# Nine heads of projection ahead of the scores, with half of the stacks and the late modulation placed later

## The chip, the cores and the metric

The kernel runs on one core of a Trainium2 chip. The metric is the device time of one execution in microseconds. The span of a profile is the time from the first to the last instruction of the program; the execution's own time is a little longer.

## The reference, cut to what matters

A transformer block on one sequence of 2048 tokens with 1024 channels, all in float32. A vector `c` gives six modulation rows, `mod = silu(c) @ w_mod`. Then:

```python
h = layernorm(x) * (1 + ca) + sa
x = x + ga * A(h)          # attention with a memory, then @ wo
h = layernorm(x) * (1 + cb) + sb
x = x + gb * B(h)          # mixer over the tokens: gelu(w1) and w2
```

`A` has 32 heads of 32 channels and cuts the tokens into 4 segments of 512. In each segment and head it computes

```python
logits = qs @ ks.T * scale + mask          # causal
a_dot = softmax(logits) @ vs
a_mem = (phi(qs) @ M) / (phi(qs) @ z + 1e-6)
o = g * a_mem + (1 - g) * a_dot
M = M + phi(ks).T @ vs;  z = z + phi(ks).sum()
```

so that a segment reads the memory `M`, `z` of those before it.

## The kernel before, in words

The work falls into two halves. The attention, to about 1000 us, ends with the products with `wo`; the mixer after it multiplies by `w1` and `w2` in a seven-product scheme for 2x2 blocks (`mix`, L927) and isn't touched by the change.

**Tiles and heads.** Four heads form a group `g` (8 of them). A tile `t` is one group on one segment: 32 tiles, first all groups on segments 0 and 1 (`pr` 0, tiles 0 to 15), then all groups on segments 2 and 3 (`pr` 1). A head's number in the loop is n = 4t + h, from 0 to 127. Matmuls take their operands in a high and a low part, so one projection is three matmuls per chunk.

**One tile's steps.** `project(t, piece)` (L378): pieces 0 and 1 make keys and values of two halves of the tokens (`nps`, 48 matmuls of 256 columns each), piece 2 transposes the keys (`kps`), makes the queries (`qps`, 24 matmuls of 512 columns), and writes both, split in high and low parts by ACT and DVE, to `sg`, of which there is one buffer. Piece 3 prepares the values (`vp`, three buffers) and reads and updates the memory (`am`, three buffers). `stack(t, h)` (L368) copies a head's rows of `sg` to its operand `sk` with three DMAs on SP (L374 to L376). There are two sets of four `sk`, so tile t's stack for head h waits until the scores of tile t - 2, head h, have read the old one. `maxima(t, h)` (L468) computes scores `sx`, `sy`, `sz` on TensorE and their row maxima on DVE; every second head transposes the maxima (`nmps`, L486) and writes their negatives into `sk` by four small DMAs (`sk<-nt`, L493). `scores(t, h)` (L507) computes the transposed scores `a0`, `a1`, `a2`, from which ACT makes exponentials `p32`; POOL masks them, ACT and POOL split them in halves `ph` and `p32`. `values(t, h)` (L533) multiplies by `vp` into the one bank `pv`; after a tile's last head the result is transposed (`ops`, L564), copied to `ot` and stored to `oT` in HBM.

**The order of the program.** The loop at L691 runs over n. In each step it issues the scores of head n, the maxima of head n + 3 (`LEADS`), the values of head n - 2 (`VL`), and projection piece m = n + 8 (`LEADP`). Stacks 0 to 2 of a tile are issued behind its piece 2, stack 3 with piece 3. Other work hangs on the steps by `plan` and `later` (a fetch at one step, its use at a later one): tokens 1024 to 2047, whose h is made from `gaw` and stored to `hT1` (steps 0 to 45), the weights of a group (`rawv`, `rawq`: fetched, split, and kept in `wsp`, from step 8g - 13), the 32 chunks of the late modulation rows (`mod_fetch` loads 512 KB `rawm`, `mod_late` reduces it on DVE: steps 49 to 56, then every second step from 60), and wo's eight parts (`wo_fetch`, `wo_split`, from step `WO0` = 65, every sixth). For m from 59 to 66 the h of segments 2 and 3 is loaded back (`reload_h`, 16 times 512 KB), the first eight of them into the pages of segment 0, as soon as its last projection has read them. At m = 123 to 130 wo's parts take the pages over.

A scheduler takes this program and sets the order on each engine by a model of the times; an engine then works its list off strictly in order, waiting on semaphores. SP issues all DMAs from one list, too, so a DMA that waits for its source or for its target's last reader holds back all behind it.

**The products with wo.** `product(tt)` (L778) loads a block of 128 tokens of `oT` as `otr` (one buffer), splits it to `ots`, and TensorE makes `po` in two halves of 24 matmuls (L797); blocks 0 to 7 need tiles of `pr` 0 alone, block 8 needs tile 30 (group 7, segment 2), block 12 needs tile 31. The first products stand between the last heads of the attention.

Of the kernel before, what the change touches and what calls it, by code (L numbers as in the profile page):

```python
# [26 lines left out]
SHIFT = 14.0 * math.log(2.0)  # L27
NV = 97
FT = F // P
LEADP, LEADS, NSK = 8, 3, 8  # L30
XB = 4
VL = 2
ML0 = 36
HB = 3
WO0 = 65
WOS = 6
WCT = 5
LEADP = 8
LEADS = 3


def attention_and_mlp(ctx, tc, x, wq, wkv, wo, beta, w1, b1, w2, b2, c, wm_a, wm_b, out):
# [320 lines left out]
    NI = len(its)  # L363
    st = {}

    last_sk, last_nt = {}, {}

    def stack(t, h):  # L368


        sk = st[t]["sk", h] = skt[t % 2][h]
        skf = sk.bitcast(F32)
        src = st[t]["sg"].bitcast(F32)[32 * h:32 * h + 32]
        SY.dma_start(skf[0:32], src[:, 0:3:2])  # L374
        SY.dma_start(skf[32:64], src[:, 0:4:3])
        last_sk[t, h] = SY.dma_start(skf[64:96], src[:, 1:3])  # L376

    def project(t, piece):  # L378
        pr, g, seg = its[t]
# [20 lines left out]
        elif piece == 2:  # L400
# [19 lines left out]
            if seg < 3:  # L420
# [3 lines left out]
                A.activation(r, r, AF.Exp, scale=-1.0)  # L424
                d["pk"] = pj.tile([P, 4, 128], F32, tag="pk", bufs=1, name=f"pk{t}")
                V.scalar_tensor_tensor(d["pk"].rearrange("p a n -> p (a n)"), kf, 0.0, r, op0=ALU.max, op1=ALU.add)
            for h in range(3):
                stack(t, h)
        else:
            stack(t, 3)  # L430
            v = d["v32"][:, :, 0:128].rearrange("p a (h e) -> p a h e", h=4)
            vp = d["vp"] = b.tile([P, 4, 4, NV], BF16, tag="vp", bufs=3, name=f"vp{t}")
            r1 = pj.tile([P, 4, 4, 32], F32, tag="tmp", bufs=2, name=f"r1_{t}")
# [240 lines left out]
        later(6 * i, lambda i=i: load_gaw(i),  # L674
              6 * i + 3, lambda r, i=i: token_tile(8 + i), "V")
    for g in range(2, NG):
        n = 8 * g - 13
        plan(n, lambda g=g: W.__setitem__((0, g), {}))
        for kind, part, n0, n1 in (("v", 0, 0, 1), ("v", 1, 1, 3), ("q", 0, 2, 4)):
            later(n + n0, lambda g=g, kind=kind, part=part: fetch_part(g, kind, part),  # L680
                  n + n1, lambda r, g=g, kind=kind, part=part: split_part(g, kind, part, r), "A")
        plan(n + 4, lambda g=g: keep_w(g))
    for j in range(32):
        n = 49 + j if j < 8 else ML0 + 2 * j + 8
        later(n, lambda j=j: mod_fetch(j), n + 1, lambda r, j=j: mod_late(j, r), "V")
    plan(WO0 - 3, lambda: spread(gaw, 0))
    for i in range(8):
        n = WO0 + WOS * i
        later(n, lambda i=i: wo_fetch(i), n + 1, lambda r, i=i: wo_split(i, r), "G")

    for n in range(-LEADS, 4 * NI + VL):  # L691
        at(scores, n)
        at(maxima, n + LEADS)
        with behind(n, "P" if n - VL >= 64 else ""):
            at(values, n - VL)
        m = n + LEADP
        if 0 <= m + 4 < 4 * NI:
            t = (m + 4) // 4
            if its[t][:2] not in W:
                with tc.issue_after(last_sk[t - 2 if t > 16 else 0, 3].ins):  # L700
                    load_w(its[t][1], its[t][0])
        if m >= 8:
            at(project, m)
        if 59 <= m < 67:
            seg, ct = 2 + (m - 59) // 4, 2 * ((m - 59) % 4)
            with ExitStack() as s:
                if seg == 3:
                    s.enter_context(tc.issue_after((last_sk[15, 3] if ct < 4 else last_nt[14, 3]).ins))
                reload_h(seg, ct)
                reload_h(seg, ct + 1)  # L710
        if 4 * NI - 5 <= m < 4 * NI + 3:
            i = m - 4 * NI + 5
            for c in (2 * (i % 4), 2 * (i % 4) + 1):
                wop[c, i // 4] = new_page(f"wo{c}_{i // 4}")
                if c < 5 or i < 4:
                    SY.dma_start(wop[c, i // 4].bitcast(F32), wos[c, i // 4])
        for f, engines in todo.pop(n, ()):
            with behind(n, engines):
                f()
# [427 lines left out]
```

## Time and profile before

| | us |
|---|---|
| median of 3 runs | 2226.57 |
| lowest and highest | 2223.17, 2226.85 |
| the profiled execution | 2224.45 |
| its span | 2222.7 |
| PE busy | 2184.5 |
| DVE busy | 1673.2 |
| ACT busy | 1132.7 |
| POOL busy | 723.6 |

The engines are PE (TensorE matmul), PEld (its weight loads), DVE (VectorE), ACT (ScalarE), POOL (GpSimd) and SP, which issues the DMAs. An engine's idle time is written in brackets behind the instruction that ends it, with what released it. The granted clock is TensorE's share of full speed. Names have lost their numbers: `sx<-sk` is any head's first maxima matmul; where the text names a tile and head, they were found by counting the instructions of that line in the program's order. A busy PE isn't PE at its peak, since a matmul's end is modelled.

### The profile page before, as it was taken

What the parts mean: (1) busy time and instruction counts of PE and PEld (TensorE: products, weight loads), DVE (VectorE), ACT (ScalarE), POOL (GpSimd) and SP (SyncE); (2) the same over time, 40 slices, a digit from 0 to 9 for tenths busy, and PEclk for the clock granted to TensorE, in tenths of its full rate; (3) what the DMA queues carried; (4) which work ended last, traced back from release to release, by engine and by line L of the source; (5) the groups of instructions that cost most, each with busy time, mean ns of one, the idle gap of its engine ahead of it and who ended that gap; (6) DMA issues with size and microseconds to landing.
All of it is one profiled execution on the core that took longest, in us unless ns stands there. A gap on an engine that the chain in (4) does not pass through costs nothing.

```text
span 2222.7 us, 38130 instructions
## 1 busy us (share of the span) xinstructions
PE 2184.5 (98%) x13786; PEld 1881.3 (85%) x13786; DVE 1673.2 (75%) x3762; ACT 1132.7 (51%) x2050; POOL 723.6 (33%) x831
## 2 busy tenths in 40 slices
PE   8999999999999999999999999999999999999999
PEld 5988998889999999888888888888888888888887
DVE  7677777767777677664858766888888887869687
ACT  5476777755666666654636533533334242424232
POOL 2165766656767677553002200033330000000000
PEclk9999999999999999999999999999999999999999
DMA  7656665587566665664754686655556541414134
GB/s 287 193 172 195 183 185 160 169 297 246 167 195 203 199 206 176 192 227 133 232 204 185 227 318 255 246 225 207 214 203 222 199 153 60 142 57 147 57 124 152
DMA packets 175184, 423.05 MB, mean 190 GB/s; under 512 B 17524, under 2 KB 71828, under 8 KB 166036
## 3 DMA queue, kind: packets, MB, share of 16 engines
q1 hardware_dynamic: 174996, 420.61, 57.4%
q8 instruction: 110, 1.80, 0.3%
q14 instruction: 78, 0.64, 0.1%
HBM read 244.62 MB, written 125.06 MB: 166 GB/s over the span
## 4 chain that ended last, share of the span: by engine, by line
PE 82%; DVE 6%; DMA 5%; ACT 3%; issue 1%; POOL 1%; SPq 1%; DVEq 0%; ACTq 0%
PE mx L927 47%; PE nps L192 10%; PE qps L200 7%; PE po L797 6%; PE pv L549 3%; DMA otr<-oT 1%; PE a L515 1%; DMA sk<-sg 1%; PE sz L478 1%; PE sx L478 1%; POOL p L531 1%; PE a L522 1%; PE sy L478 1%; PE a L518 1%; PE up L460 1%
## 5 line engine op out<-in xcount | busy, mean ns | idle before, releaser
L927 PE MATMUL mx<-bU,sp 128*128 128x512 f32 x2352 | 534.7, 389 | 1.0 <-DVE ac L934 0.9
L927 PEld LDWEIGHTS mx<-bU,sp 128*128 128x128 f32 x2352 | 441.1, 188 | 94.1 <-issue 1.3
L119 ACT CAST sp<-wr 128x384 fp32r<-128x384 f32 (+2 forms) x408 | 217.2, 545 | 433.0 <-PE mx L927 354.8
L192 PE MATMUL nps<-wv,h 128*128 128x256 f32 x3072 | 430.9, 283 | 1.1 <-DVE h L122 0.7
L927 PE MATMUL mx<-bA,sp 128*128 128x512 f32 x1764 | 430.5, 389 | 0.0
L531 POOL TENSOR_TENSOR p<-p,ph 128x640 f16<-128x640 f32 x256 | 377.7, 1476 | 121.7 <-ACT ph L529 116.8
L192 PEld LDWEIGHTS nps<-wv,h 128*128 128x128 f32 x3072 | 402.7, 190 | 8.8 <-DVE h L122 1.8
L927 PEld LDWEIGHTS mx<-bA,sp 128*128 128x128 f32 x1764 | 331.2, 188 | 68.7
L122 DVE TENSOR_TENSOR sp<-wr,sp 128x384 fp32r<-128x384 f32 (+2 forms) x408 | 259.1, 646 | 28.9 <-ACT sp L119 28.7
L934 DVE TENSOR_TENSOR ac<-mx,ac 128x512 f32<-128x512 f32 x280 | 189.4, 685 | 85.1 <-PE mx L927 84.5
L200 PE MATMUL qps<-h,wq 128*128 128x512 f32 x768 | 196.4, 399 | 0.0
L529 ACT CAST ph<-p 128x1280 f16<-128x1280 f32 x128 | 161.1, 1258 | 49.7 <-POOL p L527 49.2
L797 PE MATMUL po<-wo,ots 128*128 128x512 f32 x768 | 179.7, 391 | 1.4 <-ACT ots L119 1.4
L527 POOL TENSOR_SCALAR_AFFINE_SELECT p<-p 128x256 f32<-128x256 f32 x256 | 135.5, 535 | 119.9 <-ACT p L524 70.4
L797 PEld LDWEIGHTS po<-wo,ots 128*128 128x128 f32 x768 | 143.4, 188 | 31.2 <-ACT ots L119 1.8
L927 PE MATMUL mx<-bB,sp 128*128 128x512 f32 x588 | 164.0, 389 | 0.0
L200 PEld LDWEIGHTS qps<-h,wq 128*128 128x128 f32 x768 | 140.5, 189 | 27.1
L927 PEld LDWEIGHTS mx<-bB,sp 128*128 128x128 f32 x588 | 110.4, 188 | 22.9
L934 DVE TENSOR_TENSOR cc<-mx,cc 128x512 f32<-128x512 f32 x140 | 94.9, 684 | 41.7 <-PE mx L927 41.6
L480 DVE CUSTOM_DVE_ANT_0 sz<-sz,mask 128x512 f32<-128x512 f32 x128 | 89.2, 697 | 47.8 <-PE sz L478 46.9
L480 DVE CUSTOM_DVE_ANT_0 sx<-sx,mask 128x128 f32<-128x128 f32 (+1 forms) x256 | 93.3, 365 | 35.2 <-PE sx L478 31.5
L516 ACT ACTIVATE p<-a,shift 128x512 f32<-128x512 f32 x128 | 88.0, 688 | 43.6 <-PE a L515 39.6
(207 smaller groups left out, 3193.9 us busy)
## 6 DMA issues: line engine op xcount, KB each, us to landing
sk<-sg SPq DMA_DIRECT2D x384, 128.0 KB
wr<-in_w_dram SPq DMA_DIRECT2D x28, 1024.0 KB
wr<-in_w_dram SPq DMA_DIRECT2D x32, 768.0 KB
bstu<-ucd SPq DMA_DIRECT2D x28, 768.0 KB
wsp<-wv SPq DMA_DIRECT2D x32, 512.0 KB
rawm<-in_wm_b_dram SPq DMA_DIRECT2D x32, 512.0 KB
wv<-wsp SPq DMA_DIRECT2D x32, 512.0 KB
pcd<-cc SPq DMA_DIRECT2D x14, 1024.0 KB
```

Of the source, the lines that this page charges most:

```text
L119: last_hi[0] = A.copy(hi, src)
L122: return lo_eng.tensor_tensor(lo, src, hi.bitcast(F32), op=ALU.subtract)
L192: T.matmul(ps[:, aa], h[:, j, 128 * tt:128 * tt + 128], wt[:, i, o:o + 256], start=(n == 0), stop=(n >= 6 * NK - 2), skip_group_check=True)
L200: T.matmul(ps, wt[:, i, o:o + 128], h[:, j], start=(k + n == 0), stop=(3 * k + n == 3 * NK - 1))
L480: marks[4 * t + h - LEADS, "V"] = V.tensor_tensor_reduce(o, o, mask[:, 384 - 128 * i:], 1.0, -3.0e38, op0=ALU.add, op1=ALU.max, accum_out= ...
L516: A.activation(p32[:, 0:512], b0, AF.Exp, scale=SCALE, bias=shift)
L527: G.affine_select(w, w, pattern=[[0, 2], [1, 128]], compare_op=ALU.is_ge, fill=0.0, base=0, channel_multiplier=-1)
L529: marks[n, "A"] = A.copy(hi, p32)
L531: marks[n, "G"] = G.tensor_tensor(lo[:, c], p32[:, c], hi[:, c], op=ALU.subtract)
L797: T.matmul(ps, os_[:, i, P * ct:P * ct + P], wop[ct, nh][:, j], start=(n == 0), stop=(n == 3 * NK - 1))
L927: T.matmul(ps, ops[q][:, i, P * k:P * k + P], b[:, j], start=(m == 0 and first), stop=(m == 3 * nk - 1), skip_group_check=True)
L934: V.tensor_tensor(d, ps, d, op=ALU.add)
```

## The change

The lead of the projections goes from 8 to 9 heads: project piece m = n + 9. With it go what is counted in m (weights of a group, the reload of h, wo's pages), and the weights' fetches by step number, one step earlier. A tile's third and fourth stack (from tile 2 on) no longer follow its own pieces 2 and 3, but are issued at m = 4t + 4 and 4t + 5, ahead of that step's projection. The first eight modulation chunks are fetched at steps 58 to 65 instead of 49 to 56, the others six steps later (66 to 112), and wo's parts four steps later (from 69). The wait that the reload of segment 3 is issued behind names stack 1 of tile 15 instead of stack 3.

```diff
-LEADP = 8
+LEADP = 9
-WO0 = 65
+WO0 = 69
...
-            for h in range(3):
+            for h in range(3 if t < 2 else 2):
                 stack(t, h)
         else:
-            stack(t, 3)
+            if t < 2:
+                stack(t, 3)
...
-        n = 8 * g - 13
+        n = 8 * g - 14
...
-        n = 49 + j if j < 8 else ML0 + 2 * j + 8
+        n = 58 + j if j < 8 else 50 + 2 * j
...
         m = n + LEADP
-        if 0 <= m + 4 < 4 * NI:
-            t = (m + 4) // 4
+        t = (m - 2) // 4
+        if 2 <= t < NI and m % 4 < 2:
+            stack(t, 2 + m % 4)
+        if 0 <= m + 3 < 4 * NI:
+            t = (m + 3) // 4
...
-                    s.enter_context(tc.issue_after((last_sk[15, 3] if ct < 4 else last_nt[14, 3]).ins))
+                    s.enter_context(tc.issue_after((last_sk[15, 1] if ct < 4 else last_nt[14, 3]).ins))
```

The scheduler makes new lists from this on every engine. Three places follow. In these rows the last number of a name is a buffer's; the one or two before it are tile and head, and `wv0_5` is a weight of `pr` 0, group 5.

On TensorE, around the first maxima of tile 9. Before:

```order
L549 MATMUL pv7_1_4548<-vp7_3658,p32_7_1_4279 128x65
L478 MATMUL sx_9_0_4755<-sk1_0_501 128x128
L478 MATMUL sx_9_0_4755<-sk1_0_501 128x256
L478 MATMUL sy_9_0_4760<-sk1_0_501 128x384
L522 MATMUL a2_7_3_4527<-sk1_3_504 128x256
```

With the change:

```order
L192 MATMUL nps10_1_4737<-wv0_5_1_1_4448,h0_6_423 128x256 x3
L192 MATMUL nps10_1_4737<-wv0_5_1_1_4448,h0_7_451 128x256
L519 MATMUL a1_8_0_4675<-sk0_0_497 128x384
L192 MATMUL nps10_1_4737<-wv0_5_1_1_4448,h0_7_451 128x256 x5
L479 MATMUL sx_9_0_4806<-sk1_0_501 128x128
L479 MATMUL sx_9_0_4806<-sk1_0_501 128x256
L479 MATMUL sy_9_0_4811<-sk1_0_501 128x384
```

The maxima stood among the values of tile 7, head 1, with 24 `nps` of tile 10 between them and the last `qps` of tile 9; now they stand behind all 96 `nps` of tile 10.

On SP, at the reload of segment 2 (`h2`) and the first stack of tile 14. Before:

```order
L359 DMA h2_5_7169<-hT1_66 128x1024
L359 DMA h2_6_7292<-hT1_66 128x1024
L359 DMA h2_7_7294<-hT1_66 128x1024
L374 DMA sk0_0_497<-sg14_6788 32x2x512
L567 DMA oT_57<-ot11_6669 128x512
L375 DMA sk0_0_497<-sg14_6788 32x2x512
```

With the change:

```order
L359 DMA h2_5_7096<-hT1_66 128x1024
L374 DMA sk0_0_497<-sg14_6723 32x2x512
L375 DMA sk0_0_497<-sg14_6723 32x2x512
L376 DMA sk0_0_497<-sg14_6723 32x1024
L359 DMA h2_6_7211<-hT1_66 128x1024
L359 DMA h2_7_7213<-hT1_66 128x1024
L575 DMA rawm2_8008<-in_wm_b_dram 128x1024
```

The stack stood behind all eight loads of `h2` and behind `rawm0` to `rawm3`; now it stands behind six of them and behind `rawm0` and `rawm1`, and `rawm3` to `rawm10` come after the reload of segment 3.

On TensorE, near the end of the attention, where tile 30's result is transposed. Before:

```order
L797 MATMUL po4_0_15452<-wo1_0_14143,ots4_15445 128x512
L797 MATMUL po4_0_15452<-wo2_0_14263,ots4_15445 128x512 x3
L797 MATMUL po4_0_15452<-wo3_0_14265,ots4_15445 128x512 x3
L564 MATMUL ops30_14948<-ident_90,am30_14118 128x128 x4
L522 MATMUL a2_31_2_14964<-sk1_2_503 128x256
```

With the change:

```order
L801 MATMUL po4_0_15452<-wo7_0_14433,ots4_15445 128x512
L801 MATMUL po4_1_15478<-wo0_1_14521,ots4_15445 128x512 x3
L801 MATMUL po4_1_15478<-wo1_1_14523,ots4_15445 128x512 x3
L565 MATMUL ops30_14948<-ident_90,am30_14057 128x128 x4
L523 MATMUL a2_31_2_14964<-sk1_2_503 128x256
```

The transposes stood inside the first half of block 4's product, with 36 of its matmuls left before block 8's; now they stand inside its second half, with 18 left.

More of the change, by code (lines that the diff above doesn't have):

```diff
@@ L29 @@
 FT = F // P
-LEADP, LEADS, NSK = 8, 3, 8
+LEADP, LEADS, NSK = 9, 3, 8
 XB = 4
```

## The prediction

> **What bounds the kernel now.** I began with the page's first lines and then took the span in stretches (columns of a stretch: its length, busy time of PE, PEld, DVE, ACT, POOL with instruction counts, granted TensorE clock, DMA share, GB/s).
>
> ```profile
> span 2222.7 us, 38130 instructions
> PE 2184.5 (98%) x13786; PEld 1881.3 (85%) x13786; DVE 1673.2 (75%) x3762; ACT 1132.7 (51%) x2050; POOL 723.6 (33%) x831
> 450.00:500.00 50.00, 45.04 (x370) 40.18 (x370) 32.55 (x87) 27.34 (x51) 28.73 (x35) 0.95 0.88 299
> 550.00:600.00 50.00, 50.00 (x440) 46.46 (x440) 35.80 (x106) 32.10 (x55) 32.60 (x39) 1.00 0.51 139
> 1100.00:1150.00 50.00, 50.00 (x223) 41.40 (x222) 26.87 (x66) 19.48 (x37) 0.00 (x0) 1.00 0.65 222
> ```
>
> TensorE bounds both halves. The mixer (from 1050 us) is solid PE and none of its code is edited, so all that can change is the attention half, and there only time in which PE stands still or runs slowly. The stretch 450 to 500 us is the weakest: 5 us idle, a clock of 0.95, the most DMA.
>
> Next I took PE's waits, and the rows in time order (start, length, what, and in brackets the idle time ahead with its releaser):
>
> ```profile
> 135.16 0.47 PE L478 MATMUL sx<-sk 96*128 96x128 f32 x2 [2.33 <-issue]
> 319.53 0.47 PE L478 MATMUL sx<-sk 96*128 96x128 f32 x2 [0.74 <-DMA sk<-sg]
> 465.51 0.47 PE L515 MATMUL a<-sk 98*128 98x512 f32 x1 [0.74 <-DMA sk<-nt]
> 479.50 0.47 PE L478 MATMUL sx<-sk 96*128 96x128 f32 x2 [1.54 <-DMA sk<-sg]
> 491.29 0.61 PE L549 MATMUL pv<-vp,ph 128*128 128x97 bf16 x10 [0.43 <-ACT ph L529]
> 492.77 0.20 PE L549 MATMUL pv<-vp,p 128*128 128x65 bf16 x1 [0.87 <-POOL p L531]
> 495.10 0.51 PE L549 MATMUL pv<-vp,p 128*128 128x65 bf16 x6 [1.38 <-POOL p L531]
> 935.11 0.47 PE L478 MATMUL sx<-sk 96*128 96x128 f32 x2 [1.08 <-DMA sk<-sg]
> ```
>
> Four of them are a tile's first maxima (`sx`, head 0 of tiles 3, 9, 14 and 30, in the order of the program), which wait for the stacks; for tile 3 no releaser is named, but only four matmuls of projection part it from its `qps`. The other four lie in the weak stretch. The chain of waits there reads:
>
> ```profile
> 449.82 5.10 DMA rawm<-in_wm_b_dram
> 458.40 6.97 DMA sk<-nt
> 470.74 8.63 DMA sk<-sg
> 317.11 2.29 DMA sk<-sg
> 925.77 9.20 DMA sk<-sg
> 462.52 5.71 SPq L359 DMA_DIRECT2D h<-hT  x7
> ```
>
> A stack's DMA lands in 2.3 us when the queues are calm and in 8.6 to 9.2 us behind a burst of half-megabyte loads: modulation rows (`rawm`), weights and the reload of h. Then the stretches of 10 us show what the stall costs beyond the idle time:
>
> ```profile
> 130.00:140.00 10.00, 7.20 (x50) 6.61 (x51) 9.36 (x13) 6.94 (x11) 7.59 (x6) 0.83 1.01 297
> 470.00:480.00 10.00, 8.46 (x91) 8.12 (x88) 4.74 (x11) 4.99 (x8) 7.28 (x8) 1.00 0.84 290
> 490.00:500.00 10.00, 7.32 (x47) 6.21 (x46) 6.80 (x18) 6.25 (x12) 7.24 (x8) 0.73 0.97 358
> 500.00:510.00 10.00, 10.00 (x88) 9.55 (x88) 7.20 (x15) 5.56 (x10) 5.53 (x6) 0.93 0.72 168
> ```
>
> After two of the stalls the clock is held down: (0.17 + 0.27 + 0.07) x 10 = 5.1 us of TensorE work lost.
>
> **The change part by part.** Sums start from the profiled execution, 2224.45 us (span plus 1.75), 2.1 under the median 2226.57. No instruction is added or removed; what moves is places in queues. On SP that is 30 tiles x 2 stacks x 3 = 180 DMAs, each holding SP 0.6 us, now behind negative maxima and loads that stood after them; those go out sooner, since they no longer queue behind a stack that waits for its scores. The weights' fetches move one head with the projections that read them: nothing.
>
> *First maxima.* With nine heads of lead, all 96 `nps` matmuls of the next tile stand between a tile's last `qps` and its first `sx`; before there were 4, 24, 83 and 76 of them for tiles 3, 9, 14 and 30. One costs 0.114 us:
>
> ```profile
> 64.38 5.00 PE nps L192 x44
> ```
>
> So the stack's DMA gains 10.5, 8.2, 1.5 and 2.3 us of cover from these alone, for waits of 2.33, 0.74, 1.54 and 1.08 us. For tile 14 the queue helps as well: of the half-megabyte transfers from the last tokens' store on, 20 stood ahead of its first stack on SP, now 13, so 7 x 0.52 MB at the 358 GB/s of the row above is 10 us less to land first. All four waits go: **-5.7 us**. What is late next is the scores' wait for the negative maxima, below.
>
> *Clock.* The slow spell at 130 us follows tile 3's wait, the one at 490 us the burst. Both causes go: **-5.1 us**.
>
> *The weak stretch.* The other waits there, 0.74 + 0.43 + 0.87 + 1.38 = 3.4 us, are scores whose maxima landed 7 us late, and values behind an ACT and POOL that were held up in turn. Of the eleven `rawm` loads between the last tokens' store and the end of the reload of segment 3, two stay there and one goes just ahead; eight leave the stretch: **-3.4 us**. These loads, their `mod_late` on DVE and wo's split are not less work; they lie 6 heads (9 for the first eight) and 4 heads later, in a stretch like the 550 row, where DVE is 72% busy and DMA half. I cost them at nothing; without that cover eight DVE steps would have to be waited for, 8 x 1.2 us at most by this row (two steps):
>
> ```profile
> 512.29 2.32 DVE rawm L578 x2
> ```
>
> *Tail.* The last tile of segment 2 has to be transposed (`ops30`), stored and read back before the product of token block 8 (`po8`) can start. Columns as above:
>
> ```profile
> 1015.72 0.60 PE L564 MATMUL ops<-ident,am 128*128 128x128 f32 x4
> 1017.39 0.57 ACT L566 COPY ot<-ops 128x512 f32<-128x512 f32 x1
> 1019.11 0.38 SPq L567 DMA_DIRECT2D oT<-ot  x1
> 1023.68 0.37 SPq L781 DMA_DIRECT2D otr<-oT  x1
> 1028.36 0.73 PE L797 MATMUL po<-wo,ots 128*128 128x512 f32 x2 [1.37 <-ACT ots L119]
> 1046.27 104.55 PE po L797 x461
> ```
>
> That path takes 12.0 us from the end of `ops`, and PE waits 1.37 of them. In the new order 18 `po4` matmuls fewer stand between (18 now, 36 before), at 104.55 / 461 = 0.227 us each: 4.1 us less cover. The wait becomes 1.37 + 4.1 = 5.5 us, or 3.7 if the copy starts at once and the store isn't queued behind a load of x (1.07 and 0.72 us of slack in these rows). I take 4.5, so +3.1; and since 2.33 us of idle brought the clock down at 135 us, I add what that spell cost, 0.17 x 10 = 1.7: **+4.8 us** in all, bounds +2.3 and +5.8.
>
> The Trainium skill, "TensorE: Matmul & The Clock Gate", section "Part 1: The HAM clock gate (the "warmup" mystery)", says that the clock halves after a whole idle window of about 3.4 us, free-running. The row at 135.16, with 2.33 us of idle, disagrees with a whole idle window. By that rule a wait of 4.5 us need not hold one, the tail would cost 3.1, and the sum below would be 1.7 less.
>
> *Values.* Two values matmuls now stand close behind their own scores (tiles 5 and 11, head 2): by counting instructions 1.9 and 2.2 us. The shortest such distance now is
>
> ```profile
> 301.50 0.42 PE L522 MATMUL a<-sk 98*128 98x256 f32 x2
> 303.05 1.26 ACT L529 CAST ph<-p 128x1280 f16<-128x1280 f32 x1 [0.51 <-POOL p L527]
> 305.04 0.35 PE L549 MATMUL pv<-vp,ph 128*128 128x97 bf16 x4
> ```
>
> 3.1 us. So each waits about 1 us: **+2 us**; bounds 0 (PE may come late there anyhow) and +6, if the second half of `p` on POOL is waited for as well.
>
> *The single `sg` buffer.* A tile's third and fourth stacks still wait for the scores two tiles back, but are placed two heads later, and the next tile's write into `sg` on ACT and DVE must wait until they have landed. Behind that write on ACT are the exponentials, and PE's values wait for those. In the order of before under 5.3 us of PE work lie between those scores and the next `kps` in 3 tiles, now in 10, and in tiles 7 and 13 `kps` comes first. Issue (three at 0.6) and landing (2.3) need some 4.5. Before, ACT waited there once (answer on `sg`: us, times):
>
> ```profile
>   DMA sk<-nt: 4.2, 1
> ```
>
> The scheduler has put ACT's writes behind other work, so I take 1 us for each of tiles 7, 10 and 13: **+3 us**; bounds 0 and 3 x 4.2 = 12.6.
>
> *Three buffers.* `vp` and `am` of a tile are now rewritten one head after their last reader, before two. POOL's wait there (in sum, times, longest) is
>
> ```profile
> POOL vp L434 <- PE pv L549: 11.3, 8, 3.0
> ```
>
> and costs nothing while POOL, 65% busy in the 550 row, has the slack; bounds 0 and +3.0, one such wait on the path.
>
> Sum: -5.7 - 5.1 - 3.4 + 4.8 + 2 + 3 = -4.4, so 2224.45 - 4.4 = **2220.0 us**, 0.30% under the median.
>
> **The rivals.** *All covers hold*: nothing for values and `sg`, the tail at its lower bound: -14.2 + 2.3 = -11.9, 2212.5 us. For it: the mean distance from `qps` to `sx` grows from 11 to 18 us by counting. Against: ACT and POOL were as tight in the first half.
>
> *The clock stays up at the tail*: the wait at 479.50 left 1.00 in its row, so a wait alone need not lower it. Then the tail costs 3.1 and the time is 2218.3 us. The rule of the Trainium skill, named above, would allow this.
>
> *The wait moves*: each tile's scores need the negative maxima back in the stack. With later maxima the distance from the last maximum to its transposition falls (from 9.4 to 6.2 us on average in the first 16 tiles, and 9.9 to 5.6 after, by counting). If the first maxima no longer wait but the scores do, the 5.7 us come back: 2225.7 us. For it: the 0.74 at 465.51. Against: that one row is all there is of it.
>
> *Slower: the `sg` buffer decides.* The landing that rows show at 2.3 us rises to 7 to 9 behind loads. From about 5 us on, the seven tiles that newly fall under 5.3 us make ACT wait 4.2 us each, 29 us, and if PE passes on 45% of that (ACT is 55 to 64% busy in the 50 us rows of the attention), 13 us come on top: 2220.0 + 13 = 2233 us. For it: bursts in every second tile while weights are split. Against: three tiles had as little before, and ACT waited once.
>
> **How the numbers follow.** Forecast 2220.0 (2216 to 2222): 0.32. All covers hold: 0.12. Clock stays up: 0.08. The wait moves, from 2222.1 to 2231: 0.31. Slower: 0.17. A measurement of this kernel can tell some 0.2% from no change: 4.5 us, so faster is under 2222.1 and slower over 2231.0. Faster takes the first three, 0.52; same 0.31; slower 0.17. The range reaches from below the case with all covers to short of the slower one: 2210 to 2231, with about 0.05 left out below and 0.13 above; the upper bounds of tail, values, buffers and `sg` all together (2237.6), and those with the DVE steps, lie in what is left out.
>
> **What would show it.** In the new profile: no `sx` waiting for `sk<-sg` for over 0.5 us; clock 1.00 from 140 us to 1000 us; the former weak stretch with PE idle under 1.5 us and its longest `sk<-sg` on the chain hardly waited for; a wait of 3 to 5 us ahead of `po8` near 1015 to 1025 us, and a lowered clock behind it. ACT waiting for `sk<-sg` ahead of its `sg` write over 1 us in more than three tiles would make the slower case. PE waits in front of `a` for `sk<-nt` of over 4 us in sum would make the moved one. The forecast is wrong if the two slow-clock spells come back elsewhere in the first 500 us, or if the tail's wait is hidden.

## The result, and the profile after

| | before | after |
|---|---|---|
| median, us | 2224.56 (6 runs, 2220.15 to 2226.85) | 2231.80 (6 runs, 2230.38 to 2233.65) |
| ratio, 95% interval | | 1.0035 (1.0021 to 1.0048) |
| the profiled execution | 2224.45 | 2230.38 |

The change makes the kernel slower by 0.35%, 7 to 8 us; the forecast was 2220.0. The profiled executions differ by 5.9 us. The page of after begins:

```profile
span 2228.7 us, 38071 instructions
PE 2186.6 (98%) x13786; PEld 1883.1 (84%) x13786; DVE 1661.2 (75%) x3762; ACT 1133.7 (51%) x2050; POOL 721.2 (32%) x831
```

PE stands still for 2228.7 - 2186.6 = 42.1 us (before 38.2), and the same 13786 matmuls are busy 2.1 us longer. Where the idle time lies, a view by stretch shows (columns as in the prediction), first of before, then of after:

```profile
60.00:450.00 390.00, 379.73 (x3311) 347.02 (x3312) 282.84 (x822) 274.70 (x512) 225.95 (x261) 1.00 0.62 181
450.00:1045.00 595.00, 581.30 (x5034) 531.31 (x5034) 416.31 (x1241) 363.62 (x629) 385.13 (x458) 0.99 0.65 204
```

```profile
60.00:450.00 390.00, 381.88 (x3323) 349.05 (x3324) 282.52 (x823) 276.31 (x513) 222.46 (x259) 1.00 0.62 183
450.00:1045.00 595.00, 577.63 (x4982) 528.67 (x4983) 402.46 (x1233) 362.58 (x627) 385.16 (x458) 0.99 0.66 202
```

Up to 450 us the change saves 2.2 us of idle time (10.3 to 8.1); from there to the end of the attention it costs 3.7 (13.7 to 17.4). The other 2.4 us lie outside these stretches. 1.5 of them are in the first 60 us, where both kernels get through the same 272 matmuls (before ran them at a clock of 0.97, after at 1.00, so PE of before only looks busier), and 0.9 are in the mixer. PE's waits name the reason for the 3.7 (in sum, times, longest; the first line is before's, the others are after's):

```profile
PE a L515 <- DMA sk<-nt: 0.7, 1, 0.7
PE a L516 <- DMA sk<-nt: 9.0, 5, 3.5
PE sz L479 <- DVE mx L481: 3.1, 3, 1.9
PE po L801 <- ACT ots L119: 2.3, 1, 2.3
PE sx L479 <- DMA sk<-sg: 1.8, 2, 1.1
```

The wait of the scores for the negative maxima has grown from 0.7 to 9.0 us. The rows of after in time order, among them the first maxima of tile 14 (479.66), the scores of tiles 13, 14, 23 and 29 (the fifth wait, of 1.35 us, is tile 15's), and token block 8:

```profile
300.57 0.50 PE L479 MATMUL sz<-sk 96*128 96x512 f32 x1 [1.89 <-DVE mx L481]
479.66 0.40 PE L479 MATMUL sx<-sk 96*128 96x128 f32 x2
481.82 0.47 PE L516 MATMUL a<-sk 98*128 98x512 f32 x1 [0.87 <-DMA sk<-nt]
507.21 0.47 PE L516 MATMUL a<-sk 98*128 98x512 f32 x1 [1.42 <-DMA sk<-nt]
762.83 0.62 PE L516 MATMUL a<-sk 98*128 98x512 f32 x1 [1.93 <-DMA sk<-nt]
938.03 0.77 PE L516 MATMUL a<-sk 98*128 98x512 f32 x1 [3.47 <-DMA sk<-nt]
1033.58 0.98 PE L801 MATMUL po<-wo,ots 128*128 128x512 f32 x3 [2.29 <-ACT ots L119]
```

And the stretches of after, one of 50 us and the others of 10, with the clock in the column ahead of the DMA share:

```profile
450.00:500.00 50.00, 47.12 (x401) 42.81 (x402) 28.40 (x82) 31.66 (x56) 29.48 (x35) 0.97 0.87 267
295.00:305.00 10.00, 7.55 (x61) 6.38 (x58) 9.18 (x25) 8.28 (x19) 5.10 (x4) 0.86 0.74 210
460.00:470.00 10.00, 9.10 (x66) 8.66 (x66) 5.24 (x13) 7.69 (x12) 6.15 (x7) 0.83 0.97 322
760.00:770.00 10.00, 8.07 (x64) 7.67 (x64) 4.05 (x20) 3.31 (x7) 4.24 (x7) 0.83 0.87 294
930.00:940.00 10.00, 6.53 (x47) 6.20 (x46) 4.58 (x16) 2.92 (x5) 5.25 (x5) 0.85 0.59 162
940.00:950.00 10.00, 9.21 (x59) 8.01 (x59) 7.30 (x23) 6.74 (x13) 5.40 (x9) 0.81 0.46 128
1030.00:1040.00 10.00, 7.71 (x52) 6.31 (x50) 3.02 (x8) 4.14 (x7) 5.16 (x6) 1.00 0.64 210
```

Both old spells of lowered clock are gone, and four new ones stand beside new waits; with 0.3 that the one at 302 us loses after 305, they cost 1.7 + 1.7 + 1.7 + 3.4 = 8.5 us. That is 3.4 more than the 5.1 of before. With 1.5 us of idle time up to 1045 us (3.7 less 2.2) and the mixer's 0.9 it makes 5.8 of the 6.0 us between the two spans.

**The same moment.** At two of the four places that should have gained, one can see what became of the gain. In before, tile 29's scores start at 938.41 without a wait of their own, since PE had waited 1.08 us for the stack 3 us ahead of them; SP had issued their `nt` at 935.80, behind three stacks of tile 30:

```profile
935.18 0.53 SPq L567 DMA_DIRECT2D oT<-ot  x1
935.80 2.62 SPq L493 DMA_DIRECT2D sk<-nt  x4
938.41 0.47 PE L515 MATMUL a<-sk 98*128 98x512 f32 x1
```

In after, PE no longer waits for the stack, but `nt` is issued at 935.46, now behind tile 30's fourth stack and the store of the late modulation (`modd`):

```profile
932.79 0.60 SPq L374 DMA_DIRECT2D sk<-sg  x1
933.49 0.59 SPq L592 DMA_DIRECT2D modd<-mrow  x1
934.14 0.59 SPq L375 DMA_DIRECT2D sk<-sg  x1
934.78 0.58 SPq L376 DMA_DIRECT2D sk<-sg  x1
935.46 2.62 SPq L494 DMA_DIRECT2D sk<-nt  x4
```

The scores start at 938.03. Head 0's two DMAs are out 1.3 us behind the start of these issues and land 1.2 to 1.3 us later, so SP's queue sets that moment in both kernels.

At tile 13 the scores start 1.4 us behind the issue of their `nt` in both kernels: at 480.79 in before, just behind the 1.54 us at 479.50, and at 481.82 in after. Here SP has nothing else to issue ahead of `nt`. It waits for a load of half a megabyte to land (SP's waits from 474 us on, before and after):

```profile
SPq L493 <- DMA h<-hT: 1.9, 1, 1.9
SPq L494 <- DMA rawm<-in_wm_b_dram: 1.4, 1, 1.4
```

In the program's list that load is the eighth DMA ahead of `nt`. All 1256 DMAs of SP take eight semaphores in turn, and each issue first waits until the DMA eight places ahead of it has landed. So a load can hold up `nt` from eight places away, too. At tiles 14 and 23 it is the landing that is slow: 6.4 us behind four loads of h, and 3.5 us behind a `rawm` and a `wor`.

### The profile page after: what moved, and what is told of

Read it like the earlier page. It is cut to its first block, busy times and chain, and to the rows that moved or that the text cites. A ratio compares the mean times of both kernels' runs of the same rounds, so it can differ in the third digit from the quotient of the medians.

```text
span 2228.7 us, 38071 instructions
## 1 busy us (share of the span) xinstructions
PE 2186.6 (98%) x13786; PEld 1883.1 (84%) x13786; DVE 1661.2 (75%) x3762; ACT 1133.7 (51%) x2050; POOL 721.2 (32%) x831
## 4 chain that ended last, share of the span: by engine, by line
PE 85%; DVE 5%; DMA 4%; ACT 3%; POOL 2%; issue 1%; SPq 0%; ACTq 0%; DVEq 0%
PE mx L931 46%; PE nps L192 12%; PE po L801 8%; PE qps L200 7%; PE pv L550 3%; PE a L516 1%; PE sz L479 1%; POOL p L532 1%; PE sx L479 1%; ACT ph L530 1%; PE a L523 1%; PE a L519 1%; DVE wv L122 1%; DMA bstu<-ucd 1%; PE sy L479 1%
## 5 line engine op out<-in xcount | busy, mean ns | idle before, releaser
L528 POOL TENSOR_SCALAR_AFFINE_SELECT p<-p 128x256 f32<-128x256 f32 x256 | 125.3, 496 | 133.9 <-ACT p L525 78.7
```

Of the source, the lines that this page charges most:

```text
L528: G.affine_select(w, w, pattern=[[0, 2], [1, 128]], compare_op=ALU.is_ge, fill=0.0, base=0, channel_multiplier=-1)
```

## The experiments

**Theories.** T1: with nine heads the maxima keep their three heads of lead and stand later among the projections, which takes some 8 us from the chain maxima, `nmps`, `nt`, scores. T2: the order on SP decides when `nt` lands. Rival A names the moved third and fourth stacks as what stands ahead of `nt` there, rival B the late loads and stores of modulation and wo. The runs were made on several chips, on which the median of before lies between 2221.6 and 2224.6 us; so kernels are compared by ratio, and all ratios are to the kernel before on the same chip; "nt" and "stack" are PE's waits for `sk<-nt` and, at the maxima, for `sk<-sg` in the profiled execution (before 0.7 and 3.4, after 9.0 and 1.8); the clock is the mean of the runs' granted clock (before 0.9978 over 29 runs, after 0.9955 over 6).

One wait of one profile says little: up to 750 us the order on every engine is the same in after, e12_tile29 and e13_tile23, and the wait at tile 13 is 0.87, 1.99 and 2.89 us there, while those at tiles 13 to 15 together are 3.6 to 3.7 in all three.

| run | what it is | median us | ratio (95%) | nt | stack | clock |
|---|---|---|---|---|---|---|
| e1_lead | the lead and the stacks alone | 2225.90 | 1.0017 (1.0006 to 1.0027) | 2.7 | 0.7 | 0.9965 |
| e2_mods | the later modulation and wo alone | 2225.83 | 1.0018 (1.0008 to 1.0028) | 1.3 | 3.2 | 0.9968 |
| e3_stacks | the later stacks alone | 2237.81 | 1.0078 (1.0064 to 1.0093) | 4.9 | 6.2 | 0.9940 |
| e4_leads4 | after, maxima four heads ahead | 2222.71 | 0.9999 (0.9990 to 1.0008) | 0 | 6.2 | 0.9968 |
| e5_nt_act | after, `nt` issued by ACT | 2227.74 | 1.0028 (1.0018 to 1.0039) | 1.9 | 0 | 0.9963 |
| e6_leads4_old | e1_lead, maxima four ahead | 2225.34 | 1.0011 (1.0001 to 1.0021) | 1.6 | 7.0 | 0.9969 |
| e7_first8 | after, rows 8 to 31 at old heads | 2236.59 | 1.0067 (1.0050 to 1.0083) | 4.7 | 1.8 | 0.9945 |
| e8_before_leads4 | before, maxima four ahead | 2235.61 | 1.0058 (1.0043 to 1.0072) | 3.0 | 7.6 | 0.9940 |
| e9_fourth | after, fourth stacks behind `nt` | 2239.02 | 1.0070 (1.0052 to 1.0089) | 7.0 | 2.4 | 0.9935 |
| e10_loads_act | after, late loads issued by ACT | 2256.29 | 1.0158 (1.0138 to 1.0177) | 3.9 | 1.3 | 0.9912 |
| e11_leads4_act | e4_leads4, late loads by ACT | 2230.42 | 1.0033 (1.0017 to 1.0048) | 0 | 11.5 | 0.9967 |
| e12_tile29 | after, tile 30's fourth stack alone | 2230.15 | 1.0033 (1.0021 to 1.0046) | 7.7 | 1.5 | 0.9963 |
| e13_tile23 | after, two loads alone | 2227.34 | 1.0028 (1.0015 to 1.0041) | 5.2 | 1.5 | 0.9968 |
| e14_leads4_from12 | after, four ahead from tile 12 | 2220.85 | 0.9995 (0.9985 to 1.0004) | 0 | 2.5 | 0.9963 |
| e15_leads4_from12_old | that, without the late loads | 2219.81 | 0.9992 (0.9984 to 1.0001) | 0 | 5.1 | 0.9967 |

### The parts by themselves

```diff
 e1_lead (after); e2_mods is the same edit the other way round (before)
-WO0 = 69
+WO0 = 65
...
-        n = 58 + j if j < 8 else 50 + 2 * j
+        n = 49 + j if j < 8 else ML0 + 2 * j + 8
```

> The changed kernel with the modulation rows and wo's split back at their old heads (49+j, 44+2j and 65): what is left is nine heads of lead and the later third and fourth stacks. Theory T1 (the later place of the maxima takes about 8 us from the chain maxima, nmps, nt, scores): the waits of PE in front of a for sk<-nt stay at 5 us or more in sum, and the time is 2227 to 2233 us. Rival B (the loads that now lie in heads 58 on delay the nt transfers): the waits for sk<-nt fall under 2 us and the time is 2222 us or less.

> The kernel before with the later modulation rows and later wo alone (58+j, 50+2j, WO0 69), eight heads of lead and the stacks where they were. T1: waits for sk<-nt stay under 2 us; the weak stretch of 450 to 500 us loses part of its 5 us idle time; 2219 to 2224 us. Rival B: new waits for sk<-nt of over 4 us near 760 and 935 us, 2227 us or more.

Neither theory's numbers hold. Without the late loads the `nt` waits fall from 9.0 to 2.7 us, so most of them need the late loads (B), but the time is still 0.17% over before: new waits took their place, the longest 3.1 us for ACT's copy of the keys ahead of `kps30`. The late loads alone do what T1 said of the waits (1.3 us, the weak stretch stands still for 1.2 us where before has 5.0), and yet cost 0.18%; so the 9.0 us need the loads and the lead together. Most of what either part costs is clock: mean span times mean clock, the time at full clock, is 2216.7 and 2217.2 us for the two, where before has 2216.4. That they each cost half of the change's 0.35% fits a sum; e6_leads4_old, below, speaks against one.

```diff
 e3_stacks (before)
-            for h in range(3):
+            for h in range(3 if t < 2 else 2):
                 stack(t, h)
...
+        t = (m - 2) // 4
+        if 2 <= t < NI and m % 4 < 2:
+            stack(t, 2 + m % 4)
```

> The kernel before with the later third and fourth stacks alone, two heads later in SP's queue, eight heads of lead, modulation and wo where they were; the fetch of the weights is tied to a tile's second stack, not its fourth, as the fourth isn't placed yet there. T1: waits for sk<-nt stay under 2 us, those for sk<-sg at the third and fourth heads grow by up to 4 us; 2222 to 2228 us. Rival A (the moved stacks hold up SP, 3 x 0.6 us each, ahead of the nt transfers): waits for sk<-nt over 4 us and 2228 us or more.

Both numbers of A came (4.9 us of `nt` waits and over 2228 us), but its mechanism is only part of it. The profile shows another: DVE waits in order for a modulation row whose load stood behind the stacks on SP, and PE waits for what DVE has behind it (`am`). The rows of e3_stacks:

```profile
662.52 1.58 DVE L579 SCALAR_TENSOR_TENSOR rawm<-rawm,scb 128x1024 f32<-128x1024 f32 x1 [3.49 <-DMA rawm<-in_wm_b_dram]
664.51 0.59 PE L461 MATMUL up<-v,pk 128*128 128x132 f32 x1 [3.61 <-DVE am L455]
```

### Four heads for the maxima

```diff
 e4_leads4 (after), e8_before_leads4 (before), e6_leads4_old (e1_lead)
-LEADS = 3
+LEADS = 4
```

> The changed kernel with the maxima four heads ahead of the scores, where it has three: every maxima step stands one head earlier. T1: the waits for sk<-nt fall from 9.0 to under 2 us in sum, the spells of lowered clock at 763 and 937 us go, and some of the waits for the stacks (sx for sk<-sg) may come back; 2219 to 2225 us. Rivals A and B (SP's queue or the late loads alone decide): waits for sk<-nt of over 6 us stay and the time is 2229 to 2233 us.

T1's numbers came: no wait for `nt` is left, and 0.36%, some 8 us, is won against after (0.9999 against 1.0035). The two stretches of e4_leads4:

```profile
60.00:450.00 390.00, 376.65 (x3282) 345.03 (x3283) 277.76 (x813) 273.50 (x507) 221.82 (x256) 1.00 0.61 179
450.00:1045.00 595.00, 586.11 (x5087) 535.23 (x5087) 412.31 (x1251) 368.18 (x635) 387.36 (x462) 1.00 0.67 207
```

The second half stands still for 8.9 us (after 17.4), the first for 13.4 (after 8.1): the maxima come sooner behind the stack's load again, and the stack waits are back (6.2 us). The distance that matters can be measured: from the end of the issue of a head's two `nt` DMAs on SP to its scores on PE. For head 0 of tiles 16 to 31 it is 3.5 us on average in before and 3.4 in after, with five tiles at 1.6 or less in after, where two have so little in before; the landing alone takes 1.2 or more (the shortest of these distances). In e4_leads4 it is 8.6, 6.4 at least. So T1 falls in the form it had: the change did not shorten this distance in the second half. It was short before, and what the later maxima lost (from 11.6 to 6.7 us between the start of their last matmul and `nmps`, for heads 0 and 1 of these tiles) was slack.

> The kernel before with the maxima four heads ahead of the scores, nothing else changed. T1 and T2 (the distance from maxima to scores is short in both kernels, but before paid for it once, 0.7 us): waits for sk<-nt go to 0, waits of the first maxima for the stack (sx for sk<-sg), 5.7 us before, grow by 3 us or more, as the maxima come one head sooner behind the stack's load; 2225 to 2232 us. If four heads are simply better: 2221 us or less.

The stack waits grew, with one of 5.4 us alone, but from 5.7 (3.4 and tile 3's 2.3) to 7.6 us and so by less than the 3 expected, and the time is worse than expected. The `nt` wait did not go to 0 either (3.0 us, at tile 14). With eight heads of projections the four heads cost 0.58%, with nine they win 0.36%.

> The changed kernel with the maxima four heads ahead and with the modulation rows and wo at their old heads. If the cost of the later loads (0.18 per cent in two pairs of runs) and that of the short distance from maxima to scores are separate, it lies 0.18 per cent under the kernel with four heads alone, so 2217 to 2221 us, the time of the kernel before or up to 0.25 per cent less, without waits for sk<-nt. If the later loads cost only because that distance is short, the time is that of the kernel with four heads and the late loads, 2222 to 2225 us.

The first case was wrong on both counts: 1.6 us of `nt` waits are left, and the time is 0.12% over e4_leads4, where 0.18% under it was expected. The intervals don't tell it from e4_leads4's own time, which is the second case, 0.3 us over its range. So the 0.18% of the late loads is not there with four heads: the price of the loads depends on what else waits, and the parts can't be added up.

### SP's queue

```diff
 e5_nt_act (after)
-                last_nt[t, h] = SY.dma_start(sk[96 + part:97 + part, 0]...
+                last_nt[t, h] = A.dma_start(sk[96 + part:97 + part, 0]...
```

> The changed kernel with the negative maxima's DMAs (nt into the stack) issued by ACT, where SP issues them. Theory T2 (SP's queue decides: nt waits behind stacks, oT, weights and loads that SP has to issue first): the waits of PE in front of a for sk<-nt fall from 9.0 to under 3 us in sum and the time is 2222 to 2228 us, less what ACT loses to 256 issues. T1 (the later place of the maxima decides): these waits stay at 6 us or more and the time is 2229 us or more.

T2 held for the wait: it falls from 9.0 to 1.9 us, so it takes SP's queue to make most of it. The time lies in the range that T2 gave, at its upper end, but by ratio (1.0028 against 1.0035) it can't be told from after's. A likely reason, not tested by itself, is that ACT now waits in order ahead of these DMAs, 16.8 + 10.3 us, and what is behind it on ACT comes late.

```profile
ACT ph L530 <- DMA sk<-nt: 16.8, 9, 4.5
ACT p L520 <- DMA sk<-nt: 10.3, 3, 4.9
```

```diff
 e10_loads_act (after), e11_leads4_act (e4_leads4): rawm, wor, wos, modd
-        SY.dma_start(r, wm_b[P * j:P * j + P])
+        A.dma_start(r, wm_b[P * j:P * j + P])
...
```

> The changed kernel with the DMAs of the late modulation and of wo's split (rawm, wor, wos, modd: 32 + 8 + 16 + 2) issued by ACT, where SP issues them; the heads are as changed. If these DMAs cost by the place that they take in SP's queue ahead of nt and the stacks: the waits for sk<-nt at tiles 23 and 29 (1.9 and 3.5 us) fall under 2.5 us together, and the time is 2225 to 2228 us. If they cost by what they move (their transfers slow the landing of nt): the wait at tile 23 stays at 1.5 us or more, and the time is 2229 us or more.

> The changed kernel with the maxima four heads ahead and with rawm, wor, wos and modd issued by ACT. With four heads no scores waited for nt, so SP's queue should matter for the stacks alone (sx for sk<-sg, 6.2 us with four heads): those waits fall by 2 us or more and the time is 2216 to 2220 us, under the kernel before, if SP's queue holds the stacks; 2221 to 2225 us if the stacks wait for the scores two tiles back, which this doesn't change.

Both were wrong on the time, and in e11_leads4_act the stack waits grew to 11.5 us instead of falling (its profiled execution is the slowest of nine, 2239.88). In e10_loads_act the wait at tile 29 went with the queue; at tile 23 it stayed (2.0 us), so there the transfers themselves count. Of its 24 us over after, 13 are idle time of PE between 60 and 1045 us (38.6 against 25.5). What was not followed link by link, but fits, is that ACT has to wait for wo's split ahead of its stores (`ACT p L520 <- DMA wos<-woh` is 9.3 us in two waits). An issue moved to an engine that also computes carries its semaphore wait there. The Trainium skill, "DMA: Bandwidth & Descriptors", section "Issuing engines are not separate DMA queues", says that starting DMAs on several engines saves only the sequencer's time, "which is usually small relative to the DMA itself". Here an issue of `nt` takes 0.65 us on SP against a landing of 1.2 to 1.3, so it isn't small, and the order of the issues counts.

```diff
 e9_fourth (after); e12_tile29 has (t, m % 4) == (30, 1) as its condition
-            stack(t, 2 + m % 4)
+            with ExitStack() as s:
+                if m % 4:
+                    s.enter_context(tc.issue_after(last_nt[t - 1, 1].ins))
+                stack(t, 2 + m % 4)
```

> The changed kernel with each tile's fourth stack issued behind the negative maxima (nt) of heads 0 and 1 of the tile before, on SP, as it mostly stood in the kernel before; the modulation and wo stay late. Rival A (the moved fourth stack holds nt up, 3 x 0.6 us): the waits in front of a for sk<-nt at tiles 13, 15 and 29 (0.9, 1.4, 3.5 us) fall by up to 1.9 us each, so from 9.0 to about 4 us in sum, that of tile 23 stays, as a rawm and a wor load still stand ahead; 2226 to 2229 us. Rival B (loads and stores of the late modulation and wo decide): the sum of these waits stays over 7 us, 2230 us or more.

The sum of the waits, 7.0 us, and the time are nearer to B's. One by one, those at tiles 15 and 29 fell as rival A said (to 0.2 and 0) and that of tile 23 stayed (2.3), also as A said; that at 14 fell, too (0.4), that at 13 did not (1.1), and new ones came at tiles 20, 26 and 30 (1.0, 0.8, 1.2), one of 4.1 us for ACT's exponentials stands at 953 us, and the clock is the lowest but one of all runs. The time is 10 us over the upper end of A's range.

```diff
 e7_first8 (after)
-n = 58 + j if j < 8 else 50 + 2 * j
+n = 58 + j if j < 8 else ML0 + 2 * j + 8
```

> The changed kernel with the modulation rows 8 to 31 back at their old heads (44+2j), the first eight (58+j) and wo (from 69 on) late as in the change. Rival B in the form that the last rows and their store fall on tiles 29 and 30: the wait of 3.5 us in front of a of tile 29 goes, that of tile 23 (1.9 us) falls as its rawm load no longer stands ahead of nt, and the time is 2225 to 2229 us. If wo and the first eight decide: both waits stay and the time is 2230 us or more.

The wait at tile 29 went (0.3 us) and that of tile 23 fell (1.0), as B said, and the next link took over: tile 29's third score matmul waits 5.2 us for ACT's exponentials. The time is worse than after's. Runs e3, e7, e9 and e10 make new lists for most of the attention for the sake of a few waits; they can say where such a wait comes from, and nothing on its price.

### One place alone

The next two leave all that comes ahead of the place in its order.

> The changed kernel with the fourth stack of tile 30 alone issued behind the negative maxima (nt) of tile 29, heads 0 and 1; nothing ahead of about 930 us is reordered. If the wait at tile 29 (3.5 us) and the spell of lowered clock around it (6.8 us at half clock, 3.4 lost) are lost time, the nt DMAs start 2.5 us sooner, the wait falls under 1.5 us, and with the spell gone the time is 4 to 6 us under the changed kernel: 2224 to 2228 us where before has 2223. If the wait only moves to the next link (exponentials on ACT, the maxima of tile 30): the wait at tile 29 goes all the same, another of 2 us or more stands within 20 us of it, and the time is 2229 us or more.

The rows of e12_tile29 at the place:

```profile
933.20 2.63 SPq L494 DMA_DIRECT2D sk<-nt  x4
936.38 0.47 PE L516 MATMUL a<-sk 98*128 98x512 f32 x1 [1.89 <-DMA sk<-nt]
970.00:980.00 10.00, 7.91 (x46) 5.84 (x42) 5.58 (x26) 4.71 (x8) 8.06 (x11) 0.83 0.81 290
```

`nt` goes out 2.3 us sooner and the wait falls by 1.6, to 1.89 us, less than expected; 1.7 us are lost to a new spell of lowered clock at 974 us, behind a wait of 1.7 us ahead of the first product with `wo`, and the time is after's within the intervals. That is the time of the second expectation, though the new wait is smaller and later than it had it; of the first only the direction came true.

```diff
 e13_tile23 (after), in mod_fetch for j == 21 and in wo_fetch for i == 4
+                s.enter_context(tc.issue_after(last_nt[23, 1].ins))
```

> The changed kernel with two loads alone, modulation row 21 and wo's fifth piece, issued behind the negative maxima (nt) of tile 23, heads 0 and 1; nothing ahead of about 753 us is reordered. If these loads make the wait at tile 23 (1.9 us) by the place in SP's queue (1.2 us) and by what they move (landing 3.6 us, where 1.2 to 1.5 is enough elsewhere): the wait falls under 0.5 us, the spell at 763 us goes, and the time is 2 to 4 us under the changed kernel if what follows keeps its waits, so 2227 to 2230 us. If something else makes it: the wait stays over 1.5 us and the time is 2231 us or more.

The rows of after at the place, then those of e13_tile23:

```profile
756.73 0.58 SPq L575 DMA_DIRECT2D rawm<-in_wm_b_dram  x1
757.35 0.44 SPq L650 DMA_DIRECT2D wor<-in_wo_dram  x1
757.90 2.64 SPq L494 DMA_DIRECT2D sk<-nt  x4
```

```profile
754.66 2.61 SPq L494 DMA_DIRECT2D sk<-nt  x4
757.94 0.40 PE L516 MATMUL a<-sk 98*128 98x512 f32 x1
```

The wait is gone with its spell of lowered clock. In after two of the four DMAs were out at 759.2 and the scores started at 762.83, 3.6 us later; in e13_tile23 no more than 2.0 pass. The median, 2227.34, lies in the range expected, but after's comes from another chip; by ratio (1.0028 against 1.0035) the two cannot be told apart. So for one place alone the profile shows the gain, and the time does not.

### Room where it is short

```diff
 e14_leads4_from12 (after), e15_leads4_from12_old (e1_lead)
+def lead(k):
+    return LEADS + (k >= 48)
...
-        at(maxima, n + LEADS)
+        for k in (n + LEADS, n + LEADS + 1):
+            if n == k - lead(k):
+                at(maxima, k)
```

> The changed kernel with the maxima four heads ahead from tile 12 on and three heads ahead in tiles 0 to 11. If the short distance from nt to the scores of the second half took the gain away: the waits for sk<-nt are under 1 us in sum, the first 450 us stand still as the changed kernel does (9.3 us of PE idle from 60 to 450 us), the rest as the kernel with four heads throughout (8.9 us from 450 to 1045), so 18.2 where before has 25.3, and with a clock between the two the time is 2214 to 2220 us where before has 2222. If a stall removed is always given back at another place: 2221 us or more.

> The kernel of the run above with the modulation rows and wo back at their old heads. If the late loads cost by themselves: up to 4 us under the run above, 2212 to 2218 us. If they cost only where scores wait for nt: the same time within 2 us. If they help with four heads (as the runs with four heads throughout suggest, 2222.7 with and 2225.3 without a return to the old heads): 2 to 4 us over it.

The stretches of e14_leads4_from12:

```profile
60.00:450.00 390.00, 382.18 (x3323) 349.86 (x3323) 281.29 (x818) 276.20 (x513) 223.93 (x258) 0.99 0.62 182
450.00:1045.00 595.00, 584.84 (x5054) 533.18 (x5053) 410.83 (x1247) 366.42 (x630) 385.44 (x461) 1.00 0.67 206
```

Idle time is 7.8 + 10.2 = 18.0 us, where 18.2 was forecast and before has 24.0; no scores wait for `nt`. Up to 413 us the order on every engine is after's. So the stalls removed here weren't given back as idle time, and it was the short distance from `nt` to the scores that made the change a loss: with it mended the same change takes 0.40% less, some 9 us by ratio. Against before it isn't a gain that can be told from nothing (0.9995, 0.9985 to 1.0004), although 6 us of idle time are gone. The time, 2220.85, is 0.9 over the expectation, and the clock is lower than before's (0.9963 against 0.9980 on that chip). Without the late loads it is 2219.81 us, the lowest median of the study, ratio 0.9992 (0.9984 to 1.0001), which can't quite be told from the kernel before; the two differ by 1 us, the second of the three cases.

## Why the prediction was wrong, step by step

**The step that failed** is *First maxima*: "All four waits go: -5.7 us. What is late next is the scores' wait for the negative maxima, below." The first sentence came true: none of the four rows waits for its stack any more. The second was named and then left out of the sum. At two of the four places (tile 13's scores behind 479.50, tile 29's behind 935.11) the next link, `nt`, landed just as PE got there after its wait, and SP's issue, not PE, set its time; so PE waited there instead. The rival "the wait moves" was the right mechanism with 5.7 us given back; it measured 9.0 us of waits, 8.3 more than before, as two things came on top that the forecast had at nothing. SP's order changed (the fourth stack and `modd` ahead of tile 29's `nt`), and half-megabyte loads moved to where `nt` has to land (tile 23). The prediction had said that `nt` would go out sooner, since it no longer queues behind a stack; at tile 29 it goes out 0.3 us sooner and at tile 13 1.1 later. The rival's own sign, over 4 us of waits in front of `a`, was met, and so was one of a wrong forecast, two new slow spells in the first 500 us.

**Clock**, -5.1: the second failure. The two spells went, but four came, 8.5 us, so the term was +3.4. Forecasting that a spell goes with its stall was right; that no new stall brings one was not. How many stalls bring one is in part luck (last section).

**The weak stretch**, -3.4: idle time in 450 to 500 us fell from 5.0 to 2.9. The values' waits are gone, which was right; what is left are a wait of the moved fourth stack of tile 13 (1.1 us at 460), the `nt` of tile 13 (0.9) and smaller ones. That the late modulation and wo cost nothing was wrong: e2_mods gives them 0.18% by themselves. Most of that is a lower clock (0.9968 against 0.9978; at full clock 0.8 us are left, as above). Which stalls lower it stays open: the profiled execution of e2_mods, 2223.53, is the fastest of its 12 and doesn't show them.

**Tail**, +4.8: the wait is 2.29 us, 0.9 more than before and not 3.1, and the clock behind it is 1.00, as in the rival with +3.1. The cover fell by 4.2 us as computed (10.7 to 6.5), but the path from the end of `ops` fell, too, from 12.0 to 8.7: the copy to `ot` started at once (1.0 us less), its store went out at once (1.1 less), and the read back was issued 3.4 instead of 4.6 us behind that. The prediction had allowed for 1.8 of these 3.3 at most.

**Values**, +2: no `pv` row waits at the two places; 0. **Three buffers**, 0: POOL's wait for `pv` ahead of `vp` is 5.2 us in sum, less than before.

**The single sg buffer**, +3: ACT waited 7.4 us in four places (4.2 in one before): behind the stacks of the three tiles named, 7, 10 and 13 (0.9, 0.5 and 2.7), and of tile 14 (3.3). Over 1 us it was in two, so the slower rival's sign was not met. That ACT's wait grew by 3.2 is no proof of the 3 us, for what PE felt of it was not tested. The 4.5 us for three issues and a landing add up to 4.1 by their own figures.

**The rivals.** A slower kernel was given 17%, by the `sg` buffer; it came by the moved wait, whose upper end was put at 2231.0, and 2231.8 is 0.8 beyond that and the range.

## What to carry to other kernels

When an edit takes a wait away, look up in the trace when the *next* thing on that engine could have started without it: if its input lands at the same moment, the gain is nothing, and the place to work on is the queue that sets that moment. Slack is measured from the last hand to the consumer (here from `nt`'s issue to the scores), link by link, for a distance in heads says little. Ask, too, what SP has to see landed before it can issue: here that was the DMA eight places ahead. An edit that reorders a whole schedule tests a mechanism and not its price; a sum of idle time by stretch, with the clock beside it, comes nearer to that, and an edit at one place is clean but may be too small to be told from the noise.

## What the hardware showed beside this

**Short stalls can halve the clock, by chance of position.** The wait of 1.89 us at 300 us was followed by a lowered clock in after and e12_tile29; 1.99 us at 483 us lowered it in e12_tile29, and 2.89 us at 482 us did not in e13_tile23 (up to 750 us these three have the same order), nor did 2.29 us at 1033 us in after. The rows of e12_tile29, then of e13_tile23, each with its stretches of 3.41 us:

```profile
483.08 0.72 PE L516 MATMUL a<-sk 98*128 98x512 f32 x1 [1.99 <-DMA sk<-nt]
479.71:483.13 3.42, 1.43 (x21) 1.30 (x19) 1.53 (x7) 0.85 (x3) 1.73 (x2) 1.00 0.33 121
483.13:486.54 3.41, 3.41 (x16) 2.64 (x17) 1.10 (x3) 1.16 (x2) 0.41 (x1) 0.50 0.38 80
```

```profile
481.90 0.47 PE L516 MATMUL a<-sk 98*128 98x512 f32 x1 [2.89 <-DMA sk<-nt]
476.84:480.25 3.41, 2.18 (x27) 2.00 (x25) 1.53 (x7) 0.91 (x3) 2.52 (x2) 1.00 0.80 227
480.25:483.67 3.42, 1.77 (x16) 1.45 (x17) 0.76 (x3) 1.16 (x2) 0.03 (x1) 1.00 0.26 63
```

These stretches are steps of a grid: all slow spells of a run begin on one grid of 3.413 us and last one or more whole steps at a clock of 0.50, but for the one at the program's end (in after at 302.19, 462.62, 762.99 and 937.07 us, which are 47, 88 and 51 steps apart). The stall of e12_tile29 fell into one step, in which PE was busy for 1.43 us, and the next step was slow. The grid cut the longer stall of e13_tile23 in two, and PE was busy for 2.18 and 1.77 us of the steps. In all 17 profiles, from 60 us on, 51 of 66 spells began right after a step in which PE stood still for 45% or more; of the 10,658 steps after which the clock was full, 8 had as much. The other 15 spells began after steps with less, 22 to 44%, so the idle share of PE isn't the whole rule.

The Trainium skill, "TensorE: Matmul & The Clock Gate", section "Part 1: The HAM clock gate (the "warmup" mystery)", has a free-running window of some 3.4 us, and the clock halved after a whole idle one. The grid agrees with a free-running window; that stalls of 1.9 us are enough disagrees with a whole idle one.

**A large share of the difference is clock.** Mean span times mean clock, the time at full clock, is 2216.4 us for before (29 runs, on another chip) and 2220.1 for after: 3.7 us, while the clocks 0.9978 and 0.9955 account for some 5 us more. For e14_leads4_from12 it is 2210.4, 5 us under the 2215.6 of before on the same chip, of which the clock leaves 1 to 2. Ten executions of e13_tile23 ran from 2223.57 us (clock 0.998) to 2234.40 (0.995). Why before holds a higher clock with more idle time than e14_leads4_from12 was not found out.
